# Soft-capped attention then routed expert attention: reordering the first loads, the first transpose, the planner's early clock and two of the second stage's score blocks

## The chip, the cores and the metric

The kernel runs on one core of a Trainium2 chip. The metric is the device time of one execution in microseconds (us), a median over several executions; smaller is better. Five engines work side by side: TensorE (PE) multiplies and transposes, ScalarE (ACT) computes tanh and exp, VectorE (DVE) and GpSimd (POOL) copy and cast, SyncE (SP) issues most of the DMAs. ACT and POOL can issue DMAs too.

## The reference

```python
def _attn_ref(q, k, v, cap):                       # (8, 12, 448, 64) each, cap = 30
    scores = q @ k.transpose(0, 1, 3, 2) / sqrt(64)
    scores = cap * tanh(scores / cap)
    attn = softmax(scores)                         # over the keys
    return attn @ v

x = attn_out.transpose(0, 2, 1, 3).reshape(8, 448, 768)

def _moe_ref(x, w_gate, wq, wk, wv, wo):           # 4 experts, head size 64, the best 2 per token
    logits = x @ w_gate
    w = softmax over the 2 largest logits of each token
    for e in range(4):
        a = causal softmax of (x @ wq[e]) @ (x @ wk[e]).T / sqrt(64)
        out += (w of expert e, 0 where not chosen) * (a @ (x @ wv[e]) @ wo[e])
```

## The kernel before, in words

**Stage A** is the soft-capped attention. Its unit is a pair of heads: 6 pairs for each of 8 batches, 48 pairs in all, numbered p. For each pair, in order:

- `load(p, n)` allocates the float32 staging tiles for n pairs and issues their DMAs: `qf`, `kf` and `vf` hold the bulk; `ktf` and `vtf` hold the last 64 keys and values ("tails"), each filled by two DMAs, one per head. The staging pool has 4 buffers of each kind. Pairs 0 and 1 are loaded singly (n = 1), all later ones two pairs at a time. A load of two pairs is seven DMAs on SP's queue.
- `a_cast(p)` casts q, k and the key tails to float16 (`q16`, `k16`, `ktzs`). For pairs 0 and 1, q and the tails are cast on DVE and k on POOL; for later pairs all is on POOL. `a_castv(p)` casts the values on POOL.
- `a_tr(p)` transposes q (4 blocks), the key tails (1) and k (3) on PE into one PSUM bank, and copies them out as `qt` (two DVE copies) and `kt` (DVE; ACT for pair 0). Below it is called tr(p).
- `fill(p, i)`, i = 0 to 3, computes a block of scores on PE into one of only 2 score buffers. `tanh(p, i)` on ACT, called T(p,i) below, reads it and frees it. `expo(p, ..)`, called E(p), takes the exp of the whole pair on ACT.
- `a_pv` multiplies by the values on PE, DVE normalises, and `a_xt` transposes the result into x.

**Stage B** is the expert attention of a batch, started once its six pairs are done: the projections q, k, v, a gate, score blocks (`b_fill`), their exp on ACT (`b_exp`, called X(b,r,g) for batch b, half r, block g), and then `b_pv`, `b_ot`, `b_wo` and the stores. The last batch and what is left of the one before it are arranged by `last_batch`, a list scheduler that searches over orders.

Each engine runs its instructions in the order in which the Python code issues them. ACT's order is the list `prog`: for each pair T(p,0), E(p-1), T(p,1) to T(p,3), with the two blocks of X in between where `EXPB` says so; pair 1 alone has E(0) first. PE's order comes from class `Plan`, which keeps a modelled clock per engine: each piece of PE work has a cost, the time at which its inputs are thought ready (`plan.done`) and a due time, and is put into the gaps between the fills (`do_fill`, `pump`). What the plan gets wrong shows on the chip as PE standing in front of a piece whose input is late, with all later PE work behind it. `slot(p)` runs once per pair: it issues the loads for pair p+6, the casts for pair p+4 and two or three of the 20 weight DMAs on POOL's queue, and gives the plan its new work.

The prologue issues `load(0, 1)`, seven short matmuls that only occupy PE, `load(1, 1)`, then casts and transposes pair 0 and issues `load(2)` and `load(4)`.

Of the kernel before, what the change touches and what calls it, by code (L numbers as in the profile page):

```python
# [11 lines left out]
f16 = mybir.dt.float16  # L12
# [5 lines left out]
class Plan:  # L18
# [27 lines left out]
    def emit(self, u):  # L46
        start = max(self.pe, self.ready(u))
        u["fn"]()
        self.pe = start + u["pe"]
        end = self.pe + (self.LAT if u["aux"] != "open" and u["aux"] else 0.0)  # L50
        if u["dve"]:
            self.dve = max(self.dve, end) + u["dve"]
            end = self.dve + self.LAT
        if u["aux"] in ("open", "whole"):
            self.aux.pop(0)
        if u["aux"] == "open":
            self.opened.add(u["group"])
        self.done[u["key"]] = end
        if u["aux"] == "close":
            self.opened.remove(u["group"])  # L60
            self.done[u["group"]] = end
        if u["aux"] in ("close", "whole"):
            self.aux.append(end)

    def step(self, until, latest):


        at = {}
        for u in self.work:
            r = self.ready(u)  # L70
            if r is not None and max(r, self.pe) + u["pe"] <= latest:
# [12 lines left out]
        return True  # L84
# [156 lines left out]
def kernel(  # L241
# [13 lines left out]
    nc = tc.nc  # L255

    B, H, S, Dh = q.shape
# [3 lines left out]
    HP = H // 2  # L261
# [27 lines left out]
    def bank(shape, dtype, name):  # L289
        return bank_pool[0].tile(shape, dtype, name=name, tag=bank_pool[1])  # L290
# [3 lines left out]

    def load(p, n=2):

        if p >= NP:
            return
        b, j = divmod(p, HP)
        h0, h1 = 2 * j, 2 * (j + n)  # L300
        e2 = nc.scalar if n == 1 else nc.sync
# [6 lines left out]
        def tails(dst, src, e2=nc.sync):  # L308
            t = src[b, h0:h1, KM:S].rearrange("(j two) p d -> two p j d", two=2)
            nc.sync.dma_start(dst[0:64], t[0])  # L310
            e2.dma_start(dst[64:128], t[1])

        if p == 0:
            tails(ktf, k, e2)
        e2.dma_start(qf, q[b, h0:h1].rearrange("h (p c) d -> p h (c d)", c=QC))
        nc.sync.dma_start(kf, k[b, h0:h1, 0:KM].rearrange("h (p c) d -> p h (c d)", c=KC))  # L316
        if p:
            tails(ktf, k)
        later = [
            lambda: nc.sync.dma_start(  # L320
                vf, v[b, h0:h1, 0:KM].rearrange("h (p c) d -> p h (c d)", c=KC)
            ),
            lambda: tails(vtf, v),
        ]
        if n == 2:
            for f in later:
# [4 lines left out]
        return later  # L331

# [7 lines left out]

    warm = const.tile([128, 512], f16, name="warm")
    nc.vector.memset(warm, 0.0)
    later = load(0, 1)

    table = const.tile([128, 1], f16, name="table")
    nc.scalar.activation(table, warm[:, 0:1], AF.Tanh)
    for f in later + load(1, 1):
        f()  # L350


    ident = const.tile([128, 128], f16, name="ident")
# [17 lines left out]
    def evac(dst, src, act=False):  # L371
        (nc.scalar.copy if act else nc.vector.tensor_copy)(dst, src)  # L372
# [5 lines left out]
    def a_cast(p):  # L378
        if p >= NP:
            return  # L380
        eng = nc.vector if p < 2 else nc.gpsimd
        assert p < 8 or ("tr", p - 8) in plan.done
        assert p < 12 or ("pv", p - 12, 1) in plan.done
        qf, kf, vf, ktf, vtf = staged.pop(p)
        q16 = hd.tile([QP, QC, 2, Dh], f16, name=f"q16_{p}", tag="q16", bufs=8)
        k16 = hd.tile([128, KC, 2, Dh], f16, name=f"k16_{p}", tag="k16", bufs=8)
        for g in range(2):
            r = slice(64 * g, 64 * (g + 1))
            eng.tensor_copy(ktz[p % 8][r, r], ktf[r, :])  # L389
        nc.gpsimd.tensor_copy(  # L390
            k16, kf.rearrange("p h (c d) -> p c h d", c=KC)
        )
        eng.tensor_copy(q16, qf.rearrange("p h (c d) -> p c h d", c=QC))  # L393
        cast[p] = (q16, k16)
        vcast[p] = (vf, vtf)
        if p > 1:
            a_castv(p)
# [11 lines left out]

    def a_tr(p):  # L410
        q16, k16 = cast.pop(p)
        tps = bank([128, 1024], f16, f"tps_{p}")
        for c in range(QC):
            nc.tensor.transpose(
                tps[:, c * QP : (c + 1) * QP],
                q16[:, c, :, :].rearrange("p h d -> p (h d)"),
                ident[0:QP, 0:QP],
            )
        nc.tensor.transpose(tps[:, S : S + 128], ktz[p % 8], ident)
        for c in range(KC):  # L420
            nc.tensor.transpose(  # L421
                tps[:, S + 128 * (c + 1) : S + 128 * (c + 2)],
                k16[:, c, :, :].rearrange("p h d -> p (h d)"),
                ident,
            )
# [4 lines left out]
        m = tps[:, 0:S].rearrange("m (c p) -> m c p", c=QC)  # L430
# [4 lines left out]
        nc.vector.tensor_copy(qt[:, KM:S].rearrange("m (c t) -> m c t", c=QC), m[:, :, 96:QP])  # L435
        evac(kt, tps[:, S : S + 512], act=(p == 0))
        qkt[p] = (qt, kt)


# [453 lines left out]
    def rows(w):  # L893
        return w.rearrange("(c p) m -> p c m", p=128)
# [43 lines left out]
    def do_fill():  # L938
        nonlocal nfill
        o = reads[nfill]  # L940
        rel = ends[nfill - 2] if nfill >= 2 else 0.0
        cost = 0.42 if o[0] == "X" or o[2] else 0.19
        for d in fill_dep(o):
            plan.force(d)
        at = plan.act + sum(dur(x) for x in prog[pos : where[nfill]])
# [8 lines left out]
    t = 0.0  # L954
# [6 lines left out]
    def slot(p):  # L961

        if p % 2 == 0:
            for i in ahead(p, LOAD, DEEP):
                if i % 2 == 0:
                    load(i)
# [505 lines left out]
```

## Time and profile before

| what | us |
|---|---|
| median of 5 runs (lowest to highest) | 327.16 (326.8 to 327.78) |
| the profiled execution's own time | 326.6 |
| its span, first to last instruction | 324.9 |
| ACT busy in the span | 306.8 (94%) |
| PE busy in the span | 275.9 (85%) |
| first T starts | 8.13 |
| E(0), E(1), E(2), E(3) start | 11.19, 18.49, 24.06, 29.58 |

The span is cut into engines; an instruction's row has its start, its length, its engine and the program's line, and in brackets how long the engine had stood idle before it and what ended that. Consecutive instructions of one line can be merged into one row ("x4"). A pair that meets no wait takes 5.52 us from one E to the next (29.58 to 35.10).

### The profile page before, as it was taken

To read this page: it belongs to the slowest core of one execution; us is meant where nothing else is said; L and a number is where in the kernel's file an instruction comes from. 1 tells how busy PE (TensorE), PEld (TensorE's weight loads), DVE (VectorE), ACT (ScalarE), POOL (GpSimd) and SP (SyncE) were. 2 spreads that over 40 slices of the span, in tenths; PEclk is the share of its full clock that TensorE was granted. 3 is DMA by queue.
4 is the path that set the end of the run, shared out by engine and by line. 5 is a ranking of instruction groups with operands and counts; after the bars stand their busy time and mean duration, and the time that the engine had idled before them with its cause. 6 is when DMAs were issued, how large, how long until landed. Compare 5 with 4: busy or idle time off the path is not lost.

```text
span 324.9 us, 8764 instructions
## 1 busy us (share of the span) xinstructions
PE 275.9 (85%) x3335; PEld 177.9 (55%) x3335; DVE 213.7 (66%) x745; ACT 306.8 (94%) x306; POOL 155.5 (48%) x476
## 2 busy tenths in 40 slices
PE   5695699977899889998799879989799878998992
PEld 1263466645565565666455555657555555545761
DVE  5154446676676787689756686678866686646682
ACT  2989999999999999999999999999999999999582
POOL 3599999447707299855806384175902010021000
PEclk9569859999999999999999999999999999999998
DMA  8999999940363999689416970296012100211027
GB/s 162 242 278 235 228 225 230 204 99 1 102 168 91 280 255 270 179 207 229 102 51 195 268 174 2 97 256 160 2 49 100 26 0 2 99 48 27 2 93 249
DMA packets 65146, 46.19 MB, mean 142 GB/s; under 512 B 25872, under 2 KB 61584, under 8 KB 65104
## 3 DMA queue, kind: packets, MB, share of 16 engines
q1 hardware_dynamic: 54032, 43.58, 52.3%
q0 software_dynamic: 10512, 1.58, 6.8%
q8 instruction: 26, 0.43, 0.6%
q10 hardware_dynamic: 560, 0.48, 0.5%
q14 instruction: 16, 0.13, 0.1%
HBM read 36.19 MB, written 11.01 MB: 145 GB/s over the span
## 4 chain that ended last, share of the span: by engine, by line
ACT 77%; PE 11%; issue 5%; DMA 3%; SPq 1%; POOL 1%; DVE 1%
ACT y L477 37%; ACT p L485 30%; ACT pBs L721 9%; PE wops L803 2%; DMA ktf<-in_k_dram 1%; DMA kf<-in_k_dram 1%; PE pv L513 1%; PE kps L664 1%; PE s L461 1%; PE vps L583 1%; PE pv L507 1%; PE qps L664 1%; ACT eexp L615 1%; PE sB L702 0%; SPq L316 0%
## 5 line engine op out<-in xcount | busy, mean ns | idle before, releaser
L477 ACT ACTIVATE y<-s 128x448 f16<-128x448 f32 x192 | 153.6, 971 | 1.5 <-PE s L461 1.0
L485 ACT ACTIVATE p<-y 128x3136 f16<-128x3136 f16 (+2 forms) x49 | 142.0, 2903 | 0.0
L729 POOL TENSOR_SCALAR_AFFINE_SELECT pBs<-pBs 128x128 f16<-128x128 f16 (+1 forms) x112 | 27.8, 278 | 119.0 <-ACT pBs L721 117.4
L461 PE MATMUL s<-qt,kt 64*128 64x448 f16 x288 | 53.2, 374 | 12.2 <-ACT y L477 9.9
L513 PE MATMUL pv<-v16s,p 128*128 128x65 f16 x1152 | 60.7, 196 | 0.0
L513 PEld LDWEIGHTS <-p 128*128 128x128 f16 x1152 | 52.3, 99 | 4.4 <-issue 0.4
L507 PE MATMUL pv<-vtzs,p 128*128 128x130 f16 x192 | 43.2, 226 | 12.2 <-ACT p L485 8.2
L526 DVE TENSOR_TENSOR xk<-pv,rc 128x256 f16<-128x256 f32 x96 | 40.6, 424 | 3.3
L522 DVE RECIPROCAL rc<-pv 128x4 f32<-128x4 f32 x96 | 17.2, 180 | 38.6 <-PE pv L513 37.2
L461 PEld LDWEIGHTS <-kt 64*128 64x128 f16 x288 | 19.3, 94 | 31.3 <-issue 21.3
L372 DVE COPY ob<-wops 128x384 f32<-128x384 f32 (+1 forms) x54 | 29.9, 553 | 9.5 <-PE wops L803 9.2
L507 PEld LDWEIGHTS <-p 128*128 128x128 f16 x192 | 18.7, 98 | 29.7 <-ACT p L485 17.7
L721 ACT ACTIVATE pBs<-sB 128x960 f16<-128x960 f32 (+1 forms) x28 | 32.1, 1145 | 0.0
L583 PE MATMUL vps<-wvg,xT 128*128 128x260 f16 (+1 forms) x192 | 30.0, 275 | 0.0
L803 PE MATMUL wops<-wo,oT 128*128 128x384 f16 x128 | 29.6, 327 | 0.3 <-DVE oT L372 0.3
L393 POOL CAST q<-qf 112x512 f16<-112x512 f32 x46 | 27.9, 607 | 0.0
L390 POOL CAST k<-kf 128x384 f16<-128x384 f32 x48 | 24.1, 502 | 6.8 <-DMA kf<-in_k_dram 3.8
L401 POOL CAST v16s<-vf 128x384 f16<-128x384 f32 x48 | 24.5, 510 | 1.2 <-DMA vf<-in_v_dram 1.1
L389 POOL CAST ktzs<-ktf 64x64 f16<-64x64 f32 x92 | 21.3, 232 | 7.3 <-DMA ktf<-in_k_dram 3.1
L431 DVE COPY qt<-tps 128x384 f16<-128x384 f16 x48 | 16.8, 350 | 12.1 <-PE tps L421 12.0
L664 PE MATMUL kps<-xT,wk 128*128 128x448 f16 x96 | 24.7, 353 | 0.0
L664 PE MATMUL qps<-xT,wq 128*128 128x448 f16 x96 | 24.6, 353 | 0.0
(121 smaller groups left out, 446.9 us busy)
## 6 DMA issues: line engine op xcount, KB each, us to landing
qf<-in_q_dram SPq DMA_DIRECT2D x23, 448.0 KB, 5.5
out_dram<-ob SPq DMA_DIRECT2D x24, 384.0 KB, 2.8
kf<-in_k_dram SPq DMA_DIRECT2D x23, 384.0 KB, 6.2
vf<-in_v_dram SPq DMA_DIRECT2D x23, 384.0 KB, 5.4
ktf<-in_k_dram SPq DMA_DIRECT2D x46, 32.0 KB, 5.5
vtf<-in_v_dram SPq DMA_DIRECT2D x46, 32.0 KB, 5.2
out_dram<-ob SPq DMA_DIRECT2D x7, 192.0 KB, 2.8
qf<-in_q_dram ACTq DMA_DIRECT2D x2, 224.0 KB, 4.2
```

The source lines that it names most:

```text
L372: (nc.scalar.copy if act else nc.vector.tensor_copy)(dst, src)
L393: eng.tensor_copy(q16, qf.rearrange("p h (c d) -> p c h d", c=QC))
L461: nc.tensor.matmul(sc[:, g, 0:S], kt[r, 128 * i : 128 * (i + 1)], qt[r, :], start=True, stop=True,)
L477: nc.scalar.activation(y[(p, g)][:, o : o + n, :], score.pop((p, i))[:, 0:n, 0:S], AF.Tanh, scale=isc / capf,)
L485: nc.scalar.activation(pt[:, 0:n, :], y.pop((p, g))[:, 0:n, :], AF.Exp, scale=capf)
L507: nc.tensor.matmul(pv[:, n, :, :], pt[:, o, w : w + 128], vtz[p % 12], start=(n == 0), stop=False, skip_group_check=True,)
L513: nc.tensor.matmul(pv[:, n, g, :], pt[:, o + g, w : w + 128], v16[p % 12][:, g, j - 1, :], start=False, stop=(j == KC), skip_group_check=True,
L526: nc.vector.tensor_tensor(xt[p][:, 2 * i : 2 * i + 2, :, :], pv[:, :, :, 0:Dh], rc.broadcast_to((128, 2, 2, Dh)), ALU.mult,)
L583: nc.tensor.matmul(ps, xT[b][:, j, w : w + 128], wvg[:, j, 0 : ps.shape[1]], start=(j == 0 and first), stop=(j == NDC - 1), skip_group_che ...
L664: nc.tensor.matmul(ps, w2[r][:, j, :], xT[b][:, j, :], start=(j == 0), stop=(j == NDC - 1), skip_group_check=(b == B - 1),)
L721: nc.scalar.activation(pb[:, o0 : o0 + n], st[b].pop(("sc", r, g))[:, 0:n], AF.Exp, scale=isc)
L803: nc.tensor.matmul(ps, st[b]["oT", r][:, w : w + 128], wo2[r][:, f * (D // 2) : (f + 1) * (D // 2)], start=(r == 0), stop=(r == 1),)
```

## The change

The first four pairs are loaded singly. Pair 0's q goes first on ACT's queue and its k first on SP's, the key tails behind them; pair 1's q is on ACT's queue as before; pairs 2 and 3, which were one load of seven DMAs, become two loads of seven on SP, and `load(4)` follows them. `a_cast` casts q and k first and the tails after. For pair 0, the keys are transposed into a PSUM bank of their own. The plan doubles the cost of PE work that it places before 15 us, starts at 7.0 instead of 7.9, and gets other times for the casts. In `prog`, pair 2 joins pair 1 in having its E first. X of batch 5 moves from pairs 39 and 41 to 38 and 40, and that of batch 6 from 45 and 46 to 44 and 46.

```diff
+    COLD = 15.0
+    def pe_time(self, us, at):
+        return us * (2.0 if at < self.COLD else 1.0)
...
-        self.pe = start + u["pe"]
+        self.pe = start + self.pe_time(u["pe"], start)
...
-    later = load(0, 1)
+    first = [load(p, 1) for p in range(4)]
+    first[0][0](nc.scalar)
+    first[0][1](nc.sync)
+    first[0][3](nc.scalar)
+    first[0][2](nc.sync)
     table = const.tile([128, 1], f16, name="table")
     nc.scalar.activation(table, warm[:, 0:1], AF.Tanh)
-    for f in later + load(1, 1):
-        f()
+    first[1][0](nc.scalar)
+    for i in (1, 2, 3):
+        first[1][i](nc.sync)
+    for p in (0, 1):
+        for f in first[p][4:]:
+            f(nc.sync)
+    for p in (2, 3):
+        for f in first[p]:
+            f(nc.sync)
...
@@ load @@
+        return [
+            rows(qf, q[b, h0:h1], QC), rows(kf, k[b, h0:h1, 0:KM], KC), tails(ktf, k, 0),
+            tails(ktf, k, 1), rows(vf, v[b, h0:h1, 0:KM], KC), tails(vtf, v, 0), tails(vtf, v, 1),
+        ]
...
@@ a_cast @@
+        eng.tensor_copy(q16, qf.rearrange("p h (c d) -> p c h d", c=QC))
+        nc.gpsimd.tensor_copy(
+            k16, kf.rearrange("p h (c d) -> p c h d", c=KC)
+        )
         for g in range(2):
             r = slice(64 * g, 64 * (g + 1))
             eng.tensor_copy(ktz[p % 8][r, r], ktf[r, :])
-        nc.gpsimd.tensor_copy(
-            k16, kf.rearrange("p h (c d) -> p c h d", c=KC)
-        )
-        eng.tensor_copy(q16, qf.rearrange("p h (c d) -> p c h d", c=QC))
...
@@ a_tr @@
-        tps = bank([128, 1024], f16, f"tps_{p}")
+        qps = bank([128, 1024], f16, f"tps_{p}")
+        kps = qps[:, S : S + 512] if p else bank([128, 512], f16, "tpsk")
...
-        evac(kt, tps[:, S : S + 512], act=(p == 0))
+        evac(kt, kps, act=(p == 0))
...
-    load(2)
-    load(4)
+    for f in load(4):
+        f(nc.sync)
...
-    EXPB = {HP * (b + 1) + 3 + 2 * r - (b == B - 2) * r: (b, r) for b in range(B - 1) for r in range(2)}
+    XAT = [(3, 5)] * 5 + [(2, 4), (2, 4)]
+    EXPB = {HP * (b + 1) + o: (b, r) for b in range(B - 1) for r, o in enumerate(XAT[b])}
...
-        prog += e + t if p == 1 else t[0:1] + e + x[0:1] + t[1:2] + x[1:2] + t[2:4]
+        prog += e + t if p in (1, 2) else t[0:1] + e + x[0:1] + t[1:2] + x[1:2] + t[2:4]
...
-            plan.done[("cast", i)] = plan.act + 4.0 + 3.5 * (i - p - CAST) * (p == DEEP + 2)
+            plan.done[("cast", i)] = max(5.0 * i + 1.0, plan.act + 4.0) + 3.5 * (i - p - CAST) * (p == DEEP + 2)
...
-    plan.pe = plan.act = plan.dve = 7.9
-    plan.done.update({("cast", 1): 10.5, ("cast", 2): 14.0, ("cast", 3): 17.0, ("tr", 0): 0.0})
+    plan.pe = plan.act = plan.dve = 7.0
+    plan.done.update({("cast", 1): 8.5, ("cast", 2): 13.0, ("cast", 3): 17.0, ("tr", 0): 0.0})
```

More of the change, by code (lines that the diff above doesn't have):

```diff
@@ L70, in step @@
             r = self.ready(u)
-            if r is not None and max(r, self.pe) + u["pe"] <= latest:
+            if r is not None and max(r, self.pe) + self.pe_time(u["pe"], self.pe) <= latest:
                 at[u["key"]] = max(r, self.pe)
@@ L295, in load @@
     def load(p, n=2):
-        if p >= NP:
-            return
         b, j = divmod(p, HP)
         h0, h1 = 2 * j, 2 * (j + n)
-        e2 = nc.scalar if n == 1 else nc.sync
         qf = stage.tile([QP, 2 * n, QC * Dh], f32, name=f"qf_{p}", tag="qf")
@@ L306, in load @@
         vtf = stage.tile([128, n, Dh], f32, name=f"vtf_{p}", tag="vtf")
[L308 to L326, printed above, removed]
-                f()
         for i in range(n):
@@ L330, in load, with rows, tails @@
             staged[p + i] = (qf[:, h], kf[:, h], vf[:, h], ktf[:, i], vtf[:, i])
-        return later
+        def rows(dst, src, c):
+            return lambda eng: eng.dma_start(dst, src.rearrange("h (p c) d -> p h (c d)", c=c))
+        def tails(dst, src, i):
+            t = src[b, h0:h1, KM:S].rearrange("(j two) p d -> two p j d", two=2)
+            return lambda eng: eng.dma_start(dst[64 * i : 64 * (i + 1)], t[i])
+        return [
+            rows(qf, q[b, h0:h1], QC), rows(kf, k[b, h0:h1, 0:KM], KC), tails(ktf, k, 0),
+            tails(ktf, k, 1), rows(vf, v[b, h0:h1, 0:KM], KC), tails(vtf, v, 0), tails(vtf, v, 1),
+        ]
     LOAD, CAST, TR = 6, 4, 2
@@ L344 @@
     nc.vector.memset(warm, 0.0)
-    later = load(0, 1)
+    first = [load(p, 1) for p in range(4)]
[3 more added lines that the diff above has]
+    first[0][2](nc.sync)
     table = const.tile([128, 1], f16, name="table")
     nc.scalar.activation(table, warm[:, 0:1], AF.Tanh)
-    for f in later + load(1, 1):
-        f()
+    first[1][0](nc.scalar)
[7 more added lines that the diff above has]
+            f(nc.sync)
     ident = const.tile([128, 128], f16, name="ident")
@@ L411, in a_tr @@
         q16, k16 = cast.pop(p)
-        tps = bank([128, 1024], f16, f"tps_{p}")
+        qps = bank([128, 1024], f16, f"tps_{p}")
+        kps = qps[:, S : S + 512] if p else bank([128, 512], f16, "tpsk")
         for c in range(QC):
             nc.tensor.transpose(
-                tps[:, c * QP : (c + 1) * QP],
+                qps[:, c * QP : (c + 1) * QP],
                 q16[:, c, :, :].rearrange("p h d -> p (h d)"),
@@ L418, in a_tr @@
             )
-        nc.tensor.transpose(tps[:, S : S + 128], ktz[p % 8], ident)
+        nc.tensor.transpose(kps[:, 0:128], ktz[p % 8], ident)
         for c in range(KC):
             nc.tensor.transpose(
-                tps[:, S + 128 * (c + 1) : S + 128 * (c + 2)],
+                kps[:, 128 * (c + 1) : 128 * (c + 2)],
                 k16[:, c, :, :].rearrange("p h d -> p (h d)"),
@@ L429, in a_tr @@
         kt = hd.tile([128, 512], f16, name=f"kt_{p}", tag="kt", bufs=8)
-        m = tps[:, 0:S].rearrange("m (c p) -> m c p", c=QC)
+        m = qps[:, 0:S].rearrange("m (c p) -> m c p", c=QC)
         nc.vector.tensor_copy(
@@ L944, in do_fill @@
             plan.force(d)
+        cost = plan.pe_time(cost, plan.pe)
         at = plan.act + sum(dur(x) for x in prog[pos : where[nfill]])
@@ L965, in slot @@
                 if i % 2 == 0:
-                    load(i)
+                    for f in load(i):
+                        f(nc.sync)
         for i in ahead(p, CAST, DEEP + 2):
             a_cast(i)
-            plan.done[("cast", i)] = plan.act + 4.0 + 3.5 * (i - p - CAST) * (p == DEEP + 2)
+            plan.done[("cast", i)] = max(5.0 * i + 1.0, plan.act + 4.0) + 3.5 * (i - p - CAST) * (p == DEEP + 2)
         for _ in range(3 if p else 2):
```

## The prediction

> **What bounds the kernel now.** I read the page first (shares of busy time), then ACT's timeline from the start, the chain of waits, the windows by engine, and last the timelines of SP and POOL.
>
> ```profile
> span 324.9 us, 8764 instructions
> PE 275.9 (85%) x3335; PEld 177.9 (55%) x3335; DVE 213.7 (66%) x745; ACT 306.8 (94%) x306; POOL 155.5 (48%) x476
> PEclk9569859999999999999999999999999999999998
> ```
>
> ACT is the bound: 306.8 of 324.9 us. ACT's own work is not changed, so only its 18 idle us can shrink. ACT's timeline says where the first of them lie:
>
> ```profile
> 7.09 0.58 ACT L372 COPY kt<-tps 128x512 f16<-128x512 f16 x1 [3.55 <-DVE qt L435]
> 8.13 3.02 ACT L477 ACTIVATE y<-s 128x448 f16<-128x448 f32 x4 [0.46 <-PE s L457]
> 11.19 2.82 ACT L485 ACTIVATE p<-y 128x3136 f16<-128x3136 f16 x1
> 13.91 2.21 ACT L477 ACTIVATE y<-s 128x448 f16<-128x448 f32 x3
> 17.11 1.49 ACT L477 ACTIVATE y<-s 128x896 f16<-128x896 f32 x2 [0.99 <-PE s L461]
> 18.49 2.81 ACT L485 ACTIVATE p<-y 128x3136 f16<-128x3136 f16 x1
> ```
>
> The reader is to see a start at 8.13 and a hole of 0.99 at 17.11. E(0) to E(1) takes 7.30 against 5.52 for an undisturbed pair: 1.78 lost. From E(1) to the last E, the excess over 5.52 (7.29 with two X) adds up to only about 1.9 us. The chain of waits gives the hole's cause: key tails of the double load, POOL's cast, the transposes of pair 2, and behind them in PE's queue the fill that ACT wants.
>
> ```profile
> 9.08 4.76 DMA ktf<-in_k_dram
> ...
> 14.48 0.51 POOL k L390
> 14.99 0.57 POOL q L393
> 15.60 0.55 PE tps L414 x4
> 16.26 0.32 PE tps L421 x3
> 16.58 0.49 PE s L461 x2
> ```
>
> Windows (us; then per engine PE, PEld, DVE, ACT, POOL busy; PEclk is the granted clock):
>
> ```profile
> 14.00:16.00 2.00, 1.50 (x14) 0.96 (x15) 0.00 (x0) 2.00 (x4) 1.88 (x6) 0.50 1.03 268
> 18.00:20.00 2.00, 1.94 (x19) 1.10 (x19) 0.30 (x1) 1.98 (x3) 1.76 (x7) 0.50 1.13 274
> 262.00:282.00 20.00, 17.16 (x227) 10.87 (x225) 14.49 (x48) 20.00 (x18) 0.23 (x1) 1.00 0.09 35
> 302.50:325.00 22.50, 16.41 (x222) 11.14 (x220) 12.46 (x48) 11.45 (x28) 0.00 (x0) 0.93 0.36 124
> ```
>
> PE runs at half clock from 8 to about 21 us; it idles 2.8 us in 262 to 282, while the last 22.5 us have ACT half idle, and there the chain is PE's almost alone from 302 to 315.
>
> **The change part by part.**
>
> *Pair 0.* Before, k was issued at 1.44 behind a tail DMA at 0.80 and landed at 5.55; q (1.41, ACT's queue) at 4.9. Both now go at 0.80, so k lands 0.64 earlier, 4.9. The row: issued 0.03 apart on two queues, they landed 3.5 and 4.1 us later, against 2.2 to 3.0 for the small tails. The Trainium skill (Trainium Kernel Development and Optimization, Key Constraints) speaks against more: DMAs of all queues share the same 16 DMA engines, and a second queue saves only issue time. Were the queues independent, k could land 3.0 after issue, at 3.8, a gain of 1.75; by rule and row it is 0.64. Tails move behind the bulk: pair 1's landed 0.4 behind its k (7.1 against 6.7), so now about 5.3. Then two DVE casts (0.41, to 5.7), the tail's and three k transposes (0.11 + 0.34, ready 6.2), ACT's `kt` (0.58, to 6.9) and 0.46 to the first T: 7.35. With its own bank, `kt` no longer waits for the two `qt` copies (6.54 to 6.99, the 3.55 row). Gain 0.8; from 1.1 (tails land with k) to 0.2 (0.6 later).
>
> *Pair 2 and E(1).* The single load's q starts at 7.91 as before, but half the bytes are ahead of its tails. They were issued at 9.78 and landed at 14.1; on a near-empty queue tails took 2.3 to 2.6, so about 12.4; POOL casts q, k first (0.61, 0.51), then tails (0.51): done 13.2 against 15.54. tr(2) no longer stands before fill(1,3). With E(1) ahead of T(2,0), all of 7.35 + 3.06 (T of pair 0 as measured) + 2.72 + 2.83 + 2.70 + 2.83 + 0.43 gives E(2) at 21.95 against 24.06. Against this stands PE: in its order tr(2), fill(2,0), four a_pv halves, tr(3) and three fills fall in 14 to 22 us. The rows give 0.50 to 20 us, though PE was busy in 7.15 of the 10 us from 8 to 18. The skill's rule (TensorE: Matmul & The Clock Gate, Part 1) is that roughly 3.4 us of sustained activity frees the clock; by it PE is fast from 12 and the crowd costs nothing; by the row it is slow to 20.8, beyond the 15 that the plan now assumes. At half clock (tr 1.0, fill 0.55, a_pv half 0.43) following that order by hand costs 1.2. I take 0.6, between (bounds 0 and 1.3): E(2) at 22.5, 1.5 earlier than before, the first 0.8 included.
>
> *What is moved past: pair 4.* SP spends 0.64 us per DMA. `load(4)` was issues 19 to 25, from 12.37; two single loads make it 26 to 32, from 16.97 (where the row of `load(6)` stood), and `load(6)` goes to about 21.5.
>
> ```profile
> 12.37 0.59 SPq L315 DMA_DIRECT2D qf<-in_q_dram  x1
> 16.97 0.52 SPq L315 DMA_DIRECT2D qf<-in_q_dram  x1
> 21.61 0.84 POOL L973 DMA_DIRECT2D wq<-in_moe_wq_dram  x1
> 23.31 0.51 POOL L389 CAST ktzs<-ktf 64x64 f16<-64x64 f32 x2
> ```
>
> `load(2)` took 6.2 from first issue to last key tail (7.91 to 14.1), so pair 4's land at 23.1, cast at 23.6 (before 20.7); the plan says 21. PE will stand at tr(4) some 2.4 us with fill(3,1) behind it. Its cover is E(2), 22.5 to 25.2, which needs no PE: 23.6 + 0.6 + 0.4 + 0.2 makes T(3,1) 24.8, in time at full clock. I charge 0.3 (0 to 1.5). Then POOL: values of pair 4 at 25.5, two weight DMAs of 0.83, cast(5) at 28.8 (plan 26), tr and fill by 29.8; T(4,1) is wanted at 31.0: no cost. POOL's 5.0 to 5.2 us per pair is less than ACT's 5.52, so lateness shrinks. All 20 weight DMAs follow some 3.9 us later; second-half wq lands near 58 (37.45 + 16.7 + 3.9), wanted at 59.48 less the gain: 0.1 (0 to 0.8).
>
> *X moved up.* Same ACT work. X(6,0) must be filled by about 275; x of its batch is ready near 271 less the gain; 12 projections (2.3) and one pair's own PE work (3) just fit: 0.2 (0 to 1.2), for both batches. In return `b_wo` of batch 5 (8 x 0.33 = 2.6 on PE) can fill the idle of 262 to 272, and two `b_pv` and a `b_ot` of batch 6 leave the tail. Gain there 0.7, from 2.0 (all that idle is used) to a loss of 0.4 (the search falls worse).
>
> *Free edits.* ACT issues three loads before the first T as before (q, tails, pair 1's q at 3.05). Pair 1's tails are cast after its q, done 8.75 instead of 8.37; PE wants them at tr(1), 10.07 before, under E(0): no cost; had PE nothing else then, 0.4. The new function list, and the two more staging tiles: `load(4)` reuses pair 0's buffers, cast by 10 and needed at 17 to 21; without that cover each us late would delay pair 4 by one.
>
> **Sum** against this execution: -1.5 + 0.3 + 0.1 + 0.2 - 0.7 = -1.6, span 324.9 to 323.3, its time 326.6 to 325.0. That execution lies 0.56 under the median, so against the median 327.16: about 325.5.
>
> **The rivals.**
> (a) *Given back*: half clock and late casts eat the start; E(3) comes where it was or 0.6 sooner, tail unchanged. For it: PE at 0.50 and a plan that assumes pair 4 some 2.4 us too early. Against: E's cover. 326.5 to 327.5. This includes the case that tails landing late leave the start as it is.
> (b) *Slower: pair 4's key tails.* In 20 to 50 us, with the queue full, k loads took 9.2 us to land. If that holds at 17.6, tails land at 27, T(3,1) waits until 28.7 instead of 25.2: 3.5 lost, 328.7. It decides from a landing at 25.1 (gain gone); from 25.8 the kernel is slower. Against: these single loads ask 672 KB per 4.5 us, 149 GB/s, where the windows show 268 to 294 moved, so the queue is short at 17.
> (c) *Tail pays fully*: PE's idle in 262 to 272 is used, -2.0 there, and the crowd costs nothing: 323.6. Against: batch 6's gate and last X stay where they are.
>
> **How the numbers follow.** Forecast 0.60 (own range 324.6 to 326.4), (a) 0.18, (b) 0.10, (c) 0.12. About 0.2% (0.65 us) is what a measurement tells from no change. Faster by more than that: forecast, (c) and a little of (a), 0.74; within it 0.14, slower 0.12, mostly (b). The range 323.6 to 327.4 takes in (c), most of (a) and the bounds, and leaves out (b).
>
> **What would show it.** First T near 7.35 and `kt` waiting for PE, not DVE; no PE wait at tr(2); E(2) near 22.5; PE's wait at tr(4) ended by POOL near 23.6; POOL's first weight DMA near 25.5; from the last E's end to the span's end less than 22.4. It is wrong if ACT shows a hole of over 1 us before T(3,1) or T(4,1), if E(2) is after 23.5, or if a fill of X waits over 1 us.

## The result and the profile after

The changed kernel's median is 326.42 us (27 runs, 324.94 to 328.7) against 327.18 for the kernel before beside it (47 runs, 326.4 to 329.36): ratio 0.9974, 95% interval [0.9962, 0.9987]. It is faster by 0.8 us, where 1.6 were forecast.

The profiled execution has to be read with care. It took 327.35, which is 0.9 over its own kernel's median, and its span is 0.7 longer than that of the profiled execution before, which lay 0.6 under its median. The two profiles alone would say "slower". What they show well is where time moved, not the sum. Each profile here is one execution.

The page of the changed kernel (span; busy time and share by engine; the granted TensorE clock in tenths, in 40 slices):

```profile
span 325.6 us, 8853 instructions
PE 277.1 (85%) x3335; PEld 178.3 (55%) x3335; DVE 215.0 (66%) x745; ACT 307.2 (94%) x306; POOL 156.0 (48%) x476
PEclk9569599998999999999999999999999999999999
L483 ACT ACTIVATE y<-s 128x448 f16<-128x448 f32 x192 | 151.8, 944 | 3.0 <-PE s L463 2.4
```

ACT is still the bound, with the same work. The last row is new to the eye: ACT's idle time before its T rows is 3.0 us, 2.4 of it ended by L463, the fill of a pair's first block of scores. The clock row has a second dip, in the fifth slice (33 to 41 us), a slice earlier than before. ACT's timeline of the changed kernel says where these waits are:

```profile
6.06 0.59 ACT L376 COPY kt<-tpsk 128x512 f16<-128x512 f16 x1 [2.69 <-PE tpsk L427]
7.10 2.97 ACT L483 ACTIVATE y<-s 128x448 f16<-128x448 f32 x4 [0.45 <-PE s L463]
...
15.81 2.82 ACT L491 ACTIVATE p<-y 128x3136 f16<-128x3136 f16 x1
...
22.61 2.82 ACT L491 ACTIVATE p<-y 128x3136 f16<-128x3136 f16 x1
...
34.98 0.54 ACT L483 ACTIVATE y<-s 128x448 f16<-128x448 f32 x1 [1.56 <-PE s L463]
...
41.15 0.55 ACT L483 ACTIVATE y<-s 128x448 f16<-128x448 f32 x1 [0.36 <-PE s L463]
```

The first T starts at 7.10, the hole of 0.99 before E(1) is gone, and E(2) starts at 22.61 instead of 24.06. Then a hole of 1.56 opens before T(5,0), and one of 0.36 before T(6,0). The chain of waits of the changed kernel, followed back from that hole (start, length, what):

```profile
19.85 5.20 DMA vtf<-in_v_dram
...
25.17 0.24 POOL vtzs L410
...
25.63 0.84 POOL wq L982
...
33.96 0.29 PE tps L425
34.25 0.32 PE tps L427 x3
34.57 0.39 PE s L463
34.98 0.54 ACT y L483
```

Read from the bottom: ACT waits for fill(5,0). PE issues that behind tr(6), and tr(6) waits for POOL's cast of pair 6. POOL has hardly paused since 25.17 (0.22 us at 25.41), when the last value tail of pair 4 landed, 5.2 us after SP had issued it. Five weight DMAs, all casts of pair 5 and the q and keys of pair 6 stand between. This chain leaves out one thing that PE's rows show: PE waited for POOL for 1.00 in all, and what it then did ran at half clock (a transpose row of 0.55 and a fill of 0.58, where 0.37 and 0.35 are the rows at full clock):

```profile
33.03 0.55 PE L420 MATMUL tps<-ident,q 112*128 112x112 f16 x4 [0.63 <-POOL q L391]
...
33.96 0.29 PE L425 MATMUL tps<-ident,ktzs 128*128 128x128 f16 x1 [0.37 <-POOL ktzs L397]
...
34.36 0.58 PE L463 MATMUL s<-qt,kt 128*128 128x448 f16 x1
```

How much of the hole is each is worked out behind the experiment with POOL's first weights.

The starts of a few E's, and the tail (start of E(47) to the end of the span), for all profiled executions:

| kernel | first T | E(1) | E(2) | E(3) | E(5) | E(47) | tail | span | median |
|---|---|---|---|---|---|---|---|---|---|
| before | 8.13 | 18.49 | 24.06 | 29.58 | 40.69 | 299.42 | 25.48 | 324.9 | 327.18 |
| changed | 7.10 | 15.81 | 22.61 | 28.14 | 41.59 | 300.97 | 24.63 | 325.6 | 326.42 |
| changed, again | 7.03 | 15.73 | 22.73 | 28.26 | 41.57 | 301.29 | 24.26 | 325.5 | 326.37 |
| casts planned later | 7.21 | 15.91 | 23.07 | 28.59 | 39.63 | 299.68 | 24.93 | 324.6 | 326.33 |
| X not moved | 7.46 | 16.21 | 22.81 | 28.33 | 40.55 | 300.54 | 24.98 | 325.5 | 326.53 |
| one load | 7.10 | 15.80 | 22.71 | 28.24 | 39.78 | 299.08 | 24.66 | 323.7 | 325.41 |
| one load, again | 7.49 | 16.25 | 22.81 | 28.33 | 39.95 | 298.85 | 24.58 | 323.4 | 326.28 |
| shared bank | 8.14 | 16.89 | 23.22 | 28.74 | 40.35 | 300.04 | 24.68 | 324.7 | 326.44 |
| one load, pair 2's order undone | 7.35 | 17.89 | 24.63 | 30.15 | 41.23 | 300.55 | 24.84 | 325.4 | 328.01 |
| one load, full-clock plan | 7.45 | 16.88 | 23.62 | 29.14 | 40.33 | 299.87 | 25.27 | 325.1 | 326.12 |
| one load, X not moved | 7.44 | 16.19 | 23.32 | 28.84 | 40.32 | 299.31 | 24.97 | 324.3 | 326.02 |
| first weights later | 6.90 | 15.60 | 22.86 | 28.38 | 39.73 | 304.72 | 24.30 | 329.0 | 328.28 |
| before + pair 2's order | 8.22 | 18.44 | 26.63 | 32.16 | 43.46 | 302.00 | 25.49 | 327.5 | 327.74 |
| before + single loads | 8.12 | 17.92 | 28.48 | 34.00 | 45.31 | 303.85 | 25.58 | 329.4 | 331.42 |

Against before, the changed kernel's profile is 1.44 ahead at E(3), 0.90 behind at E(5), 1.55 behind at E(47), and gets 0.85 back in the tail: 0.7 longer in all.

### The profile page after: what moved, and what is told of

It is laid out like the page before. It is cut to its first block, busy times and chain, and to the rows that moved or that the text cites. A ratio compares the mean times of both kernels' runs of the same rounds, so it can differ in the third digit from the quotient of the medians.

```text
span 325.6 us, 8853 instructions
## 1 busy us (share of the span) xinstructions
PE 277.1 (85%) x3335; PEld 178.3 (55%) x3335; DVE 215.0 (66%) x745; ACT 307.2 (94%) x306; POOL 156.0 (48%) x476
## 4 chain that ended last, share of the span: by engine, by line
ACT 73%; PE 10%; issue 5%; DMA 4%; POOL 3%; SPq 3%; DVE 1%; POOLq 0%
ACT y L483 35%; ACT p L491 29%; ACT pBs L727 9%; SPq L318 2%; DMA vtf<-in_v_dram 2%; PE wops L809 1%; DMA vf<-in_v_dram 1%; PE pv L519 1%; DMA qf<-in_q_dram 1%; SPq L314 1%; PE kps L670 1%; PE vps L589 1%; PE qps L670 1%; POOL q L391 1%; PE s L467 1%
## 5 line engine op out<-in xcount | busy, mean ns | idle before, releaser
L483 ACT ACTIVATE y<-s 128x448 f16<-128x448 f32 x192 | 151.8, 944 | 3.0 <-PE s L463 2.4
L467 PE MATMUL s<-qt,kt 64*128 64x448 f16 x288 | 52.0, 371 | 11.7 <-ACT y L483 8.6
L519 PE MATMUL pv<-v16s,p 128*128 128x65 f16 x1152 | 61.4, 196 | 0.0
L519 PEld LDWEIGHTS <-p 128*128 128x128 f16 x1152 | 53.2, 100 | 3.6 <-issue 0.4
L376 DVE COPY ob<-wops 128x384 f32<-128x384 f32 (+1 forms) x52 | 28.7, 553 | 10.7 <-PE wops L809 10.1
L513 PEld LDWEIGHTS <-p 128*128 128x128 f16 x192 | 18.9, 99 | 29.9 <-ACT p L491 17.1
L727 ACT ACTIVATE pBs<-sB 128x960 f16<-128x960 f32 (+1 forms) x28 | 31.1, 1112 | 0.4 <-PE sB L708 0.4
L589 PE MATMUL vps<-wvg,xT 128*128 128x260 f16 (+1 forms) x192 | 29.0, 275 | 0.0
L405 POOL CAST v16s<-vf 128x384 f16<-128x384 f32 x48 | 24.4, 508 | 6.0 <-DMA vf<-in_v_dram 3.2
L410 POOL CAST vtzs<-vtf 64x64 f16<-64x64 f32 x96 | 22.8, 237 | 3.8 <-DMA vtf<-in_v_dram 1.0
L670 PE MATMUL kps<-xT,wk 128*128 128x448 f16 x96 | 23.6, 353 | 0.0
```

What stands on the lines that cost most here:

```text
L467: nc.tensor.matmul(sc[:, g, 0:S], kt[r, 128 * i : 128 * (i + 1)], qt[r, :], start=True, stop=True,)
L483: nc.scalar.activation(y[(p, g)][:, o : o + n, :], score.pop((p, i))[:, 0:n, 0:S], AF.Tanh, scale=isc / capf,)
L513: nc.tensor.matmul(pv[:, n, :, :], pt[:, o, w : w + 128], vtz[p % 12], start=(n == 0), stop=False, skip_group_check=True,)
L519: nc.tensor.matmul(pv[:, n, g, :], pt[:, o + g, w : w + 128], v16[p % 12][:, g, j - 1, :], start=False, stop=(j == KC), skip_group_check=True,
L589: nc.tensor.matmul(ps, xT[b][:, j, w : w + 128], wvg[:, j, 0 : ps.shape[1]], start=(j == 0 and first), stop=(j == NDC - 1), skip_group_che ...
L670: nc.tensor.matmul(ps, w2[r][:, j, :], xT[b][:, j, :], start=(j == 0), stop=(j == NDC - 1), skip_group_check=(b == B - 1),)
```

## The experiments

All ratios are to runs of the kernel before beside them (median 327.03 for casts later, X not moved, one load and shared bank; 327.25 for the two repeats and the two edits of the kernel before; 327.23 for the rest). With 5 to 12 runs each, an interval is 0.7 to 2.2 us wide, so two experiments that differ by less than about 1 us are told apart by their traces only.

**Pairs 2 and 3 in one load.** This takes back the two single loads and leaves everything else.

```
-    first = [load(p, 1) for p in range(4)]
+    first = [load(0, 1), load(1, 1), load(2, 2)]
-    for p in (2, 3):
+    for p in (2,):
```

> The changed kernel with pairs 2 and 3 loaded together again by seven DMAs, so that the load of pair 4 starts near 12 us instead of 16. My theory (the two single loads are what makes the casts of pairs 4 to 7 late): the first T stays at 7.1, PE waits 0.5 to 0.8 at tr(2) for POOL under E(1), cast(4) is done near 20.7, cast(6) near 31, and the hole of 1.56 at T(5,0) is gone: 1 to 2 below the changed kernel. Rival (single loads pay): cast(2) near 15.5 opens a hole at T(2,0) of 1 us or more, and the time is that of the changed kernel or above it.

Measured: 325.41 (6 runs), ratio 0.9949 [0.9930, 0.9968], 1.0 below the changed kernel. E(2) is at 22.71, so the early arrival of pair 2 alone had bought nothing there. POOL issues its first weight DMA at 21.82 instead of 25.63, and E(5) is at 39.78: of the lead of 1.3 at E(3), 0.9 is left. Since the gap of 1.0 was at the edge of the intervals, both kernels ran again side by side.

**The same and the changed kernel, again.**

> One load for pairs 2 and 3 once more, to be set against the changed kernel in the same call. Theory A (the two single loads cost SP 7 more issues of 0.64 us, so pairs 4 and later arrive 2 to 4 us later at POOL): E(5) near 39.8, 0.7 to 1.3 us under the changed kernel's median. Theory B (the 1.0 between the two medians of the last call was chance): within 0.4 of it.

> The changed kernel once more, beside its version with one load for pairs 2 and 3 on the same chip. Its profiled execution had 1.56 us of ACT idle before T(5,0), behind a value tail of pair 4 that landed at 25.2; another execution of the same instruction stream up to pair 36 had E(5) at 40.55 instead of 41.59. Theory A (the late landing is an accident that moves POOL's whole backlog): E(5) between 40.3 and 41.6 and the hole between 0.3 and 1.6, median 326.2 to 326.7. Theory B (the hole is in every execution): E(5) at 41.4 to 41.8.

Measured: one load 326.28 (12 runs; 326.09 without one of 330.04), ratio 0.9972 [0.9954, 0.9990]; changed kernel 326.37 (12 runs), 0.9972 [0.9948, 0.9996]. The traces repeat: E(5) at 39.95 with one load, 41.57 with two. The medians do not: the 1.0 has become 0.1 to 0.3, as theory B has it. That single loads cost 1 us in the median is therefore not shown; that its two traces lose more from E(3) to E(5) (2.4 and 2.3) than the two with one load (0.5 and 0.6) is; two other profiles with single loads, X not moved and shared bank, lose 1.2 and 0.6. The changed kernel's second profile is the first over again, with the value tail cast at 25.17:

```profile
25.17 0.24 POOL L410 CAST vtzs<-vtf 64x64 f16<-64x64 f32 x1 [0.83 <-DMA vtf<-in_v_dram]
...
34.96 0.55 ACT L483 ACTIVATE y<-s 128x448 f16<-128x448 f32 x1 [1.43 <-PE s L463]
```

**Casts planned 3 us later.** The planner believes in a cast time of at least `5.0*i + 1.0`; cast(6) was to be done at 31 and was done at 33.9. With later times it puts fill(5,0) ahead of tr(6).

```
-            plan.done[("cast", i)] = max(5.0 * i + 1.0, plan.act + 4.0) + ...
+            plan.done[("cast", i)] = max(5.0 * i + 4.0, plan.act + 4.0) + ...
```

> The changed kernel, but the plan takes the cast of pair i from 4 on as done at 5i+4 instead of 5i+1; nothing else. My theory: in the changed kernel's trace PE stood at tr(6) until 33.96 with fill(5,0) behind it, because the plan has cast(6) at 31 and POOL finished it at 33.9; that cost ACT 1.56 us before T(5,0) and 0.36 before T(6,0). Then this kernel has no such hole, E(4) near 33.7 and a time some 1.5 to 2.2 below the changed kernel. Rival 1, the half clock from 32 to 42 us is what costs: the holes stay, time within 0.4 of the changed kernel. Rival 2, POOL itself is too late for ACT: the holes stay at T(5,0) with PE's wait ended by POOL.

Measured: 326.33 (9 runs), ratio 0.9972 [0.9949, 0.9996]. The two holes are gone from ACT's timeline (E(4) at 34.11, E(5) at 39.63). PE's timeline of this kernel shows the reason: the fill that ACT wants, L463, is issued 2.6 us ahead of tr(6), L420, and waits for nobody but ACT:

```profile
33.10 0.53 PE L463 MATMUL s<-qt,kt 128*128 128x448 f16 x1 [0.35 <-ACT y L483]
...
35.71 0.44 PE L420 MATMUL tps<-ident,q 112*128 112x112 f16 x4
```

With this order half clock costs ACT nothing here: the fill's row of 0.53 is of half clock too. That the order alone removes the hole is not shown, for POOL also came earlier in this execution: its first weight DMA is at 24.17 instead of 25.63, and the cast of pair 6 was done at 32.42, about when PE had finished the fills ahead of it. The span is 1.0 shorter than that of the changed kernel's profile, but that one lay 0.9 over its median; the median moved only 0.1, and the expected time was missed. Of the 1.96 won at E(5), 0.67 is lost again by E(47) (0.25 from E(5) to E(6), 0.30 from E(11) to E(12)), and 0.3 in the tail.

**POOL's first weights later.** The same hole from POOL's side: 0, 3, 4, 4 weight DMAs in the first four slots instead of 2, 3, 3, 3.

> The changed kernel (single loads for pairs 2 and 3), with POOL's first two weight DMAs (2 x 0.83 us, at 25.6 in the profile) issued behind later pairs' casts: 0, 3, 4, 4 in the first four slots instead of 2, 3, 3, 3. Theory A (POOL runs without a gap from about 24 on, so what it issues ahead of the casts of pairs 5 and 6 delays tr(6), which stands before fill(5,0)): casts of pairs 5 and 6 end 1.7 earlier, no PE wait for POOL at tr(6), ACT's hole before T(5,0) under 0.4 against 1.56, E(5) at 39.6 to 40.2 against 41.59, median 325.4 to 326.0. Theory B (PE's half clock between 30 and 40 us makes the hole): casts earlier, hole still over 1, E(5) after 41, median as the changed kernel's 326.4. If the second-half weights become late instead, a wait for wq of 1 us or more shows near 60 to 66 us.

Measured: 328.28 (12 runs), ratio 1.0025 [0.9992, 1.0058]. The first half came as theory A has it: although the value tail of pair 4 was late here too (cast at 25.08), the cast of pair 6 was done at 31.95, there is no PE wait at tr(6), and E(5) is at 39.73. The rest is the edit's own price: with four weight DMAs in a row the cast of pair 8 comes late, and the queue fills up. PE's and POOL's timelines of this kernel:

```profile
42.77 0.56 PE L420 MATMUL tps<-ident,q 112*128 112x112 f16 x4 [2.16 <-POOL q L391]
...
49.05 0.53 POOL L982 DMA_DIRECT2D wo<-in_moe_wo_dram  x1 [2.32 <-DMA wvg<-in_moe_wv_dram]
```

PE stands 2.16 at tr(8). POOL's issue at 49.05 waited until an older weight had landed, so the cast of pair 9 is late as well, and PE stands 2.37 at tr(9) with the fill behind it. ACT loses 1.52 and 3.11. POOL's backlog cannot simply be pushed back, and the time that was hoped for did not come.

**What the hole is made of.** Eight of the profiles have the same order of PE there: tr(6) stands before fill(5,0), and tr(7) before fill(6,0). They differ in when POOL was done and in PE's clock. The row of the four q transposes shows the clock: 0.37 us at full, 0.55 to 0.56 at half. "Lost" is the time from one E to the next, less 5.52.

| kernel | cast of pair 6 ends | PE's wait for POOL at tr(6) | q row of tr(6) | lost, E(3) to E(4) | q row of tr(7) | lost, E(4) to E(5) |
|---|---|---|---|---|---|---|
| changed | 33.91 | 1.00 | 0.55 | 1.76 | 0.56 | 0.65 |
| changed, again | 33.89 | 0.87 | 0.56 | 1.62 | 0.56 | 0.65 |
| X not moved | 32.61 | none | 0.56 | 0.71 | 0.56 | 0.47 |
| shared bank | 32.33 | none | 0.37 | 0.00 | 0.56 | 0.57 |
| first weights later | 31.95 | none | 0.55 | 0.31 | 0.37 | 0.00 |
| one load | 30.08 | none | 0.56 | 0.51 | 0.37 | 0.00 |
| one load, again | 30.47 | none | 0.37 | 0.00 | 0.56 | 0.57 |
| one load, X not moved | 30.05 | none | 0.56 | 0.43 | 0.37 | 0.00 |

PE waited for POOL at tr(7) in none of them. So with a cast in time and PE at full clock nothing is lost with this order; at half clock 0.3 to 0.7 is lost per pair, however early POOL is; and PE's wait for POOL comes on top. Of the 2.4 that the changed kernel's profile loses from E(3) to E(5), late casts are about 1.0 to 1.5 (its 1.76 less the 0.3 to 0.7), and half clock is the rest, with all of the second pair's 0.65. PE's row at tr(6) of "shared bank", then that of "one load", and under it the row of ACT that waited in the second:

```profile
32.76 0.37 PE L420 MATMUL tps<-ident,q 112*128 112x112 f16 x4
```

```profile
32.43 0.56 PE L420 MATMUL tps<-ident,q 112*128 112x112 f16 x4
```

```profile
33.82 0.54 ACT L483 ACTIVATE y<-s 128x448 f16<-128x448 f32 x1 [0.32 <-PE s L463]
```

Why PE fell to half clock in some of these stretches and not in others was not found.

**Pair 2's order undone** (with one load): the first T of pair 2 goes back ahead of E(1).

```
-        prog += e + t if p in (1, 2) else ...
+        prog += e + t if p == 1 else ...
```

> Pairs 2 and 3 in one load, and the first read of pair 2 back ahead of E(1). Compared with the kernel that has only the one load (325.41, E(1) at 15.80, E(2) at 22.71, E(3) at 28.24). Theory A (the order is what makes the start earlier: with E(1) ahead of T(2,0) ACT needs pair 2 a whole E of 2.8 us later): E(1) waits for tr(2) and fill(2,0), so E(1) near 18.0, E(2) near 23.5, E(3) near 29.0; 0.5 to 0.9 us slower, 325.9 to 326.3. Theory B (what comes after E(3), PE's half clock and the casts, sets the pace whatever the start is): E(5) and the time unchanged, 325.2 to 325.6.

Measured: 328.01 (12 runs; 327.95 without one of 332.47), ratio 1.0028 [1.0007, 1.0050]: slower than before, and 1.7 to 2.6 behind the two medians with one load. ACT's timeline has the wait of the kernel before, now 1.38:

```profile
17.45 0.54 ACT L483 ACTIVATE y<-s 128x448 f16<-128x448 f32 x1 [1.38 <-PE s L463]
```

PE runs tr(2) at 15.00, and fill(2,0) at 16.86, with 0.88 of waiting for DVE's `kt` in between; E(1) stands behind it. This loses 1.6 to 2.1 at E(1) and 1.8 to 1.9 at E(2) against the two profiles with one load. The expectation had E(1) right, and E(2) and the time 1.1 and 1.7 too early.

**Before with pair 2's order only.**

> The kernel before with one edit: E(1) ahead of the first read of pair 2. Theory A (this order is what carries the gain at the start: undone in the kernel with one load it cost 2.1 at E(1) and 2.6 in the median): first T still 8.13, E(1) at 16.8 to 17.2 against 18.49, E(2) at 23.0 to 23.6 against 24.06, median 325.9 to 326.6. Theory B (it works only with the earlier casts and the doubled costs of the other edits): the fill of T(2,0) still comes late and ACT waits after E(1) as long as it did before it, E(2) at 24.0 or later, median 327.0 to 327.6.

Measured: 327.74 (12 runs), ratio 1.0022 [1.0005, 1.0039]: theory A fails. E(1) is where it was (18.44) and E(2) 2.6 later. ACT's timeline:

```profile
17.49 0.92 ACT L477 ACTIVATE y<-s 128x896 f16<-128x896 f32 x1 [1.32 <-PE s L461]
18.44 2.82 ACT L485 ACTIVATE p<-y 128x3136 f16<-128x3136 f16 x1
...
24.35 2.39 ACT L477 ACTIVATE y<-s 128x896 f16<-128x896 f32 x3 [1.86 <-PE s L461]
```

The old cast times still put tr(2) ahead of the last fill of pair 1, and tr(4) ahead of the fills of pair 2: PE stands 0.77 at tr(2) and 1.17 at tr(4) for POOL. So the order alone does not help; it needs something of the other edits. The plan's times for the casts are what this trace points to, but they were not tried alone.

**Before with single loads only.** Pairs 2 and 3 as two loads of seven DMAs on SP's queue, all else as before.

> The kernel before with one edit: pairs 2 and 3 as two single loads. Theory A (single loads delay pair 4 and all behind it; pair 2's own arrival was not what E(1) waited for longest): SP issues pair 4 at 17 instead of 12.4, E(1) 0.3 to 0.9 earlier than 18.49 as pair 2's key tails land earlier, but E(5) at 41.2 to 42.5 against 40.69, median 327.6 to 328.6. Theory B, the prediction's (pair 2's early landing is worth more than the 0.3 that late pairs cost): E(1) at 17.5, gain kept, median 326.0 to 326.6.

Measured: 331.42 (5 runs), ratio 1.0128 [1.0104, 1.0152], 4.2 us slower. Theory A has the sign, but it expected 327.6 to 328.6. E(1) comes 0.57 earlier, so pair 2's early arrival is worth that. Then PE's timeline, and under it the row of ACT that waited:

```profile
19.46 0.33 PE L421 MATMUL tps<-ident,k 128*128 128x128 f16 x3
24.42 0.56 PE L414 MATMUL tps<-ident,q 112*128 112x112 f16 x4 [4.64 <-POOL q L393]
...
26.64 0.55 PE L461 MATMUL s<-qt,kt 64*128 64x448 f16 x2
```

```profile
27.24 1.35 ACT L477 ACTIVATE y<-s 128x896 f16<-128x896 f32 x2 [4.90 <-PE s L461]
```

Directly after tr(3), PE stands 4.64 us at tr(4), with the fills that ACT wants behind it. POOL began on pair 4's key tails at 22.72 here and at 22.22 in the changed kernel. The old cast order does q and k behind the tails, done at 24.37, and the new one does them ahead, all done at 22.75: that accounts for 1.6 of the 4.90 (0.5 by the later arrival, 1.1 by the order of the casts). The rest, as far as the two traces show, goes with the orders of PE and ACT: the changed kernel's PE comes to tr(4) at 21.94, behind fill(3,0), and ACT has E(2) to do meanwhile; there PE waits 0.50 and ACT not at all.

**Keys of pair 0 in the shared bank.**

```
-        kps = qps[:, S : S + 512] if p else bank([128, 512], f16, "tpsk")
+        kps = qps[:, S : S + 512]
```

> The changed kernel with pair 0's keys transposed into the same PSUM bank as its q. My theory: the copy of kt on ACT waits for the two copies of qt on DVE again. These end near 6.2 in the changed kernel and kt started at 6.06, so the first T moves by 0.15 to 0.6 and the time by as much. Rival (the bank was the main gain of the start): the first T goes back by 0.8 or more.

Measured: 326.44 (12 runs), ratio 0.9981 [0.9969, 0.9992]. The first T is at 8.14. Here PE's first transposes and fills are at half clock (rows of 0.55), as in the kernel with X not moved, whose first T is at 7.46: like against like, the bank is worth 0.7 of the 1.03 that the first T gained, more than the 0.15 to 0.6 expected, and about 0.3 is left for the other edits at the start, the order of the loads first. ACT's row of this kernel:

```profile
6.91 0.58 ACT L376 COPY kt<-tps 128x512 f16<-128x512 f16 x1 [3.54 <-DVE qt L441]
```

`kt` waits for DVE's second `qt` copy again, although k's cast began at 4.51 (4.47 in the changed kernel, 5.61 before). Yet E(3) is only 0.60 later, E(5) is 1.24 earlier, and the median is the same. A gain at the first T is not a gain at the end.

**The plan at full clock** (with one load): `COLD = 0.0`.

> One load for pairs 2 and 3, and the planner counts PE at full clock from the start (COLD 0 instead of 15). Matmul rows show PE at half speed to about 20.8 us. Theory A (the doubled costs make the planner put less PE work ahead of the reads that ACT wants): without them a_pv halves slip ahead of fills of pairs 1 and 2, ACT idles 0.5 to 1.0 more before 21 us, E(2) at 23.2 to 23.7, time 325.9 to 326.4. Theory B (the order before 21 us has so little choice that the cost constants do not matter): E(2) within 0.2 of 22.71, time 325.2 to 325.6.

Measured: 326.12 (12 runs), ratio 0.9965 [0.9949, 0.9981]. E(1) and E(2) are 0.6 to 1.1 and 0.8 to 0.9 later than in the two profiles with one load, as theory A has it; an a_pv half and tr(2) go ahead of the last fill of pair 1 and ACT idles 0.48 before it. In the median this is not told apart from one load (325.41 and 326.28).

**X not moved**, once with two loads and once with one: `XAT = [(3, 5)] * 6 + [(3, 4)]`.

> The changed kernel with X of batches 5 and 6 back at pairs 39, 41, 45 and 46. My theory: moving them up shortened the stretch from the last E to the end from 25.5 to 24.6 us at a cost of 0.2 to 0.4 in the pairs before; then this kernel is 0.4 to 0.8 slower than the changed one, with the stretch near 25.5. Rival: the last schedule's search merely fell differently; then it is within 0.3 of the changed kernel.

> One load for pairs 2 and 3, with the last two batches' X back at their old places (3 and 5, 3 and 4). Theory A (the move shortens the tail by the 0.7 that was forecast): last E to the end 25.3 to 25.5 instead of 24.62, its two charges of 0.3 at E(39) and E(45) gone, time 325.9 to 326.1. Theory B (the moves cost before the tail about what they save in it; with two loads the undone move gave 326.53 against 326.42): tail 24.9 to 25.0, time within 0.3 of 325.41.

Measured: 326.53 (12 runs), ratio 0.998 [0.9959, 1.0001], and 326.02 (8 runs), 0.9958 [0.9941, 0.9974]. The tails are 24.98 and 24.97, against 24.63 and 24.26 (two loads) and 24.66 and 24.58 (one load): 0.3 to 0.7 less with the move. But edits that leave X alone shift the tail as much: with the move it is 24.93 when the casts are planned later and 25.27 with the full-clock plan. The rival, that the search for the last schedule merely fell differently, is not excluded. The move adds 0.29 at E(39) and 0.30 at E(45), which are gone with one load and the move undone. In the medians its net is near zero: 0.1 with two loads, and with one load 326.02 lies between the two medians of the kernel that has the move.

## Why the prediction was right, and where it was not

The sign, the places and the first half of the sum held. Predicted 325.5 against 326.42; the forecast gain of 1.6 came out as 0.8, with an interval of 0.4 to 1.2. None of the prediction's signs of being wrong came up, because the hole opened one pair later, before T(5,0), than it looked for one. That the median lands so near the forecast is in part luck: in the profiles a loss that was not in the sum eats the gain, and the median must have less of it.

- *Pair 0.* First T 7.35 forecast, 7.10 and 7.03 measured, `kt` waiting for PE as said. The working was off in its shares: it took the gain from the earlier landing of k (its cast began 1.14 earlier, where 0.64 was forecast), and the bank came in as a by-product. The bank turned out to be worth 0.7 and the rest about 0.3, for the `qt` copies were the last wait ahead of `kt`.
- *Pair 2 and E(1).* E(2) 22.5 forecast, 22.61 and 22.73 measured, no PE wait at tr(2). The crowd on PE was charged 0.6 on top of 5.96 from E(1) to E(2); it took 6.80, so the charge should have been 0.84, nearer to the order followed by hand at half clock (1.2) than to the full-clock rule (0). What carries E(2) is the order together with the other edits: either without the other is slower than before (1.0028 and 1.0022). Doubling the costs is worth 0.6 to 1.1 at E(1) and no measured time. The single load, which the prediction counted in, was not needed for it.
- *What is moved past.* Pair 4: PE's wait at tr(4) was forecast at some 2.4 and was 0.50, for the new plan puts it later; no cost on ACT. First weight DMA at 25.5 and cast(5) at 28.8 forecast, 25.63 and 28.87 measured. The step that failed is the next one: "no cost", and "POOL's 5.0 to 5.2 us per pair is less than ACT's 5.52, so lateness shrinks". The casts of pairs 5, 6 and 7 start 5.03 apart, so it shrinks by 0.5 us a pair, too slowly: tr(6) is placed ahead of fill(5,0), as tr(7) is ahead of fill(6,0), and these have no E in front of them as cover. The cost came one pair later than the prediction's working goes. The term of 0.3 measured 1.76 from E(3) to E(4) and 0.65 from E(4) to E(5) in the trace. Late casts are 1.0 to 1.5 of that. The rest is a second thing that the sum put at nothing: PE fell back to half clock at 31.4, after the prediction had taken it to be fast from 21 us on.
- *X moved.* 0.2 forecast for both batches; 0.29 at E(39) and 0.30 at E(45) measured, together 0.6, within its bounds of 0 to 1.2.
- *The tail.* 0.7 forecast, 0.85 and 1.22 measured. But 0.5 of it is there without the move, so that the number was met is luck.
- *Weights.* No projection waited for the second-half wq. In its place an excess that the prediction did not have: 0.70 at E(10) in the changed kernel (X waits 0.37 for its fill), 0.93 at E(12) in the second profile. It goes with PE's clock: nine of the fourteen profiles lose 0.6 to 1.1 at E(10) or E(12), and all nine have PE at half clock for some 3.3 us just there (by the rows, 72.4 to 75.6 us in the changed kernel); the five without the loss do not.
- *The rivals.* (a), given back, has the time of the two profiled executions of the changed kernel (327.35 and 327.25); the median lies just under its lower end. Its account is not theirs: it has E(3) at most 0.6 sooner and the tail unchanged, and they have 1.3 to 1.4 and 0.85 to 1.22. (b) did not happen in the changed kernel, and its mechanism is real: it is what the kernel before does with single loads, 4.2 slower. Its point of decision was wrong. It was put at a landing of 25.1, and 22.7 was enough with PE's old order and q cast last.
- *A sum.* The excess over 5.52 and 7.29 from E(1) to the last whole E is 2.5 in the profile before, not 1.9. Nothing rests on it.

What stays open is the sum. In each profile of the changed kernel the loss after E(3) is larger than the gap between forecast and median, and no kernel with that loss repaired has a median clearly below 326.4: one load gave 325.41 and then 326.28, the later casts 326.33. One reason may be that the executions are of two kinds, told apart by the mean granted clock (below). Under 0.972 the changed kernel has a median of 327.46 (13 runs) and one load 325.45 (5 runs); over it they have 326.00 (26 runs) and 326.30 (12 runs, the one of 330.04 left out). So in the first kind single loads go with 2.0 us, as the profiles have it, and in the second with none. Of the first 6 runs with one load, 3 were of the first kind, and of the next 12 only 2, which may be how 1.0 became 0.1. This split was made after the fact and no run tests it. Why the last value tail of pair 4 was cast only from 25.1 on in three executions, and both value tails by 24.4 in three others with the same order of loads, was not found. No version tried is shown to beat the changed kernel.

## What to carry to other kernels

In a queue with a fixed order, ask of every instruction that may wait what stands behind it: with arrivals half a microsecond apart, a late operand cost ACT nothing in one kernel and 4.9 us in another, where the wanted fill stood behind the waiting transpose and ACT had no other work. When a start is made earlier, follow the lead past the first milestone (here E(2) and E(3)) to the next engine that runs without pause: here POOL, which had the same backlog as ever, and then PE, whose clock fell. An order with no slack loses to either. When a chain of waits suggests one cause, set all traces of the same order side by side: here that gave about half of the loss to PE's clock, which the chain does not show. Edits can need each other: the new order without the rest, and the rest without the new order, each made this kernel slower.

## What the runs showed of the hardware

- A clock record can be blind at the start. In the kernel with X not moved, the granted clock reads 1.00 from 8 to 20 us, yet its fills take 0.55 to 0.56 us there, as in the changed kernel, which shows 0.50 (0.36 at full clock). The length of a matmul row is the safer reading. The rows of the first kernel:

```profile
16.97 0.55 PE L463 MATMUL s<-qt,kt 128*128 128x448 f16 x1 [0.88 <-DVE kt L376]
...
21.82 0.35 PE L463 MATMUL s<-qt,kt 128*128 128x448 f16 x1
```

- In all these profiles PE is at half clock up to 19 to 26 us. In the changed kernel it is busy for 6.92 of the 10 us from 10 to 20, but with pauses of up to 1.15 us until 16.56; from there it works on, and is at full clock 4.7 us later. In the fourteen profiles full clock came 2.9 to 6.0 us after the last pause of over 0.15 us:

```profile
16.56 0.55 PE L463 MATMUL s<-qt,kt 128*128 128x448 f16 x1 [0.88 <-DVE kt L376]
...
21.26 0.23 PE L513 MATMUL pv<-vtzs,p 128*128 128x130 f16 x1
```

- The Trainium skill (TensorE: Matmul & The Clock Gate, Part 1) has roughly 3.4 us of sustained activity free the clock. These rows are of that size and do not contradict it. The prediction applied it to a stretch with pauses, and so had PE fast from 12 by the rule; counted from the last pause, it would be about 20 (an estimate: 16.56 and that figure).
- In the changed kernel PE fell back to half clock at 31.4, though its longest pause since 22.8 was 0.91 us, and again at 72.4 (windows: us, PE busy, granted clock, DMA share, GB/s). What makes it fall was not found:

```profile
32.00:40.00 8.00, 5.94 (x52) 0.50 1.48 215
72.00:76.00 4.00, 4.00 (x61) 0.57 0.05 13
```

- The mean granted clock of a run goes with its time in the changed kernel, by a split that was made after seeing the data. Of its 39 runs, the 13 under 0.972 have a median of 327.46 and the other 26 one of 326.00; in the kernel before it is 327.05 (27 runs) and 327.36 (59). Both profiled executions of the changed kernel are of the first kind (0.957, 0.958), so they look worse than its median. In the profiles the kinds differ from the start: the eight with a mean of 0.943 to 0.960 have the first transposes at full clock (rows of 0.37), the six with 0.978 to 0.989 at half (0.55 to 0.56), and these are the ones whose record is blind there, which alone lifts the mean by some 0.02 (an estimate: 12 of 325 us at half clock). The cause is not known.
- POOL's DMA queue can hold up the engine: with weights bunched, an issue waited 2.32 us until an older weight had landed.
